# Remainders of at most 64 rows, row indices first, and a tail of nested steps in a kernel for attention and two expert layers

## The chip, the cores and the metric

One core of a Trainium2 chip. The metric is the device time of one execution in microseconds (us); the median of three runs of the kernel before is 681.71 us (680.21 to 682.52).

## The reference

Three layers follow one another. An attention over 2 x 8 heads, 768 positions and 64 features lets a query see the keys of its own hash bucket alone. A feed-forward layer of 1536 tokens (512 to 2048 to 512) has a rational function between its products. The last layer sends each token to the one expert of eight whose logit is highest:

```python
e_idx = np.argmax(logits, axis=1)
for e in range(E):
    mask = e_idx == e
    h = np.maximum(x[mask] @ w1[e], 0.0)
    ye = h @ w2[e]
    out[mask] = gate_w[mask, None] * eom[mask, e, None] * ye
```

w1 is 512 x 1024 and w2 1024 x 512 for each expert. How many tokens an expert gets is known only on the chip.

## The kernel before, in words

Every fp32 operand is split into two fp16 parts, so that one product of the reference is three on TensorE. The operations of attention, the feed-forward layer and the first expert block are recorded in a graph, each with its engine and cost; a planner on the host (order) goes through them in simulated time and emits, per engine, the ready operation with the lowest rank in the table PLACES. What stands behind it, `tail()`, is written out by hand and follows the graph on every engine's queue.

**Routing.** The tokens of an expert are cut into pairs (256 rows, two blocks or subs of 128) and at most one rest. VectorE counts (slots, cum at L872 to L878), makes the matrices SO and SR (L886, L887), and TensorE turns them into row numbers with inv() (L937, L943). idg (L938) is the list for the gathers, idx (L939) that for the scatters, cs_ (L945) the scales. Between these lie the operations that find the expert of each pair and rest (es, L947 to L963; regs is what SyncE loads) and the flags (flf, flc, fli, L964 to L970), two bits for each pair and rest: not empty, and for a rest a second half block of 64 rows, for a pair a new expert.

**Movement.** gather (L984, GpSimd, software queue) fetches rows of x2d into a buffer XG, and a transposing DMA on SyncE (turn, L987) puts it into XGT. Buffers 0 and 1 serve even steps, 2 and 3 odd steps, 4 and 5 the rests. load_chunk (L794, SyncE) brings one of eight chunks (512 KB) of an expert's weights into the staging buffer st; a register from regs picks the expert, and a condition leaves out the load where a pair keeps its expert or a slot is empty. ScalarE and VectorE convert st to the fp16 parts WH (L1002) and WL (L1005), one set for the pairs and one for the rests. Results go out with an indirect scatter on GpSimd (L1042 for a pair's sub, L1117 for a rest); each waits until the one before it has landed.

**The steps.** Pair 0 is in the graph. tail() begins with the rest-0 gather, its eight weight loads and its transpose, then loads fli into registers on every engine. Step k (1 to 9) treats pair k and rest k-1:

```python
gather(k + 1, 0), gather(k + 1, 1); gather_rest(k)
whole(k)          # from k = 3 inside If(pair_over(k, 0)), with an Else
renew(k + 1, 0, 4); load_rest(k, 0, 4)
for sub in range(2): scale_out(k, sub), scatter(k, sub)
If(rest_over(r, 0)): rest(r, 0); If(rest_over(r, 1)): rest(r, 1)
renew(k + 1, 4, 8); load_rest(k, 4, 8)
```

whole(k) converts half of the rest's weights, runs the first products of both subs together with 256 columns (up_pair, 96 matmuls, L1077; relus at L1082 and L1083), issues turns(k) for the next step, converts the other half and runs the second products (mm2s, 48 matmuls of 512 columns, L1034). rest(r, hh) has 96 first products of 64 columns (L1094) and 24 second ones (L1107), then ScalarE and VectorE (L1115, L1116) make its output. Steps above 4 are nested in If(steps > k). renew converts the pair's weights where the expert changes. In this execution five pairs (steps 1 to 5) ran behind pair 0, and rests 0 to 3 in steps 1 to 4, each with its first half block alone.

Of the kernel before, what the change touches and what calls it, by code (L numbers as in the profile page):

```python
# [21 lines left out]
NB, NR = 10, 8  # L22
# [34 lines left out]
    "uiuougusv7u@u@vDuSucu&u<u]u_v5v9vJueu>u|v%v;v#v/v}w4w8xPxrxNxfx%x%x%tjtpr#r(r;r?r{s2s4s8sEsAsMsSsYsis!s.t7tJtPtXr^s0s6sCsUsIscsOsysss+s]t1t9tLtTt=u~vBvNq]r3r9rJrhrXrrrxr%rzr*r=r[r}"  # L57
    "smsuvTvZvfwKs&s<s|t3tBtFtHtNtZtRtltxt(t;t{u8wSwgwowqw!w.xVx1y2y8tftvt#t}uGuUukuwu)uyv3vFvRvbvlvtv-w2wEwat*uYumuuu+u:vXvjvvvhv(w0wAwQwewmwww$w<w]uEu$u.vHvVvPv*vpv[v?w6wIwcwuw*w:w~x3"
    "xBxFvnvrvzv=wGwOwywYw@w+x5xHxRxbxlxuxzx#x*x/x?x^y0yCyKyOyQySyWycygymyYyuy+y:yeyky|zfzlz?yqyyy$y$y.y_y_y_ywy!y)y>y<y~zFzFzFzFz7zDzNzTzZznzxzp!4z[!8!C!Gy@y@z3zBzLzRzbzXzjz-z-z-z-zVzV"
    "z#z#z#z#z#z#z%z;wCw&wUx9v1v^wivdwsw_uqwWx7vLwkxhwMxJx-v{w>x=u!w|xXvxxDxxxLxTxZxdxnx(xpxvx;x[x}y4x{y6yAyUyiysy&y]z9zJyEyGyIyMyayoxjz5zHzPzdz*zhztz(z/z^z{z}!0!6!Az=!Ezr!2"  # L60
# [257 lines left out]
def kernel_body(ctx, tc, qt_, kt_, v, proj, wio, ab, wg, w1, w2, cst, out):  # L318
# [398 lines left out]
    def switch():  # L717
# [24 lines left out]
        flf, flc, fli = tp(p2, "flf", [1, 2, NIT]), tp(p2, "flc", [1, 3]), tp(p2, "fli", [1, 3], I32)  # L742
        nc.gpsimd.memset(flf[:, 1, 2 * NR:], 0.0)
# [4 lines left out]
        P["pw"] = pw = tp(p2, "pw", [128, NB - 1])  # L748
        for j in range(NB - 1):
            nc.gpsimd.memset(pw[:, j:j + 1], 4.0**j)  # L750
# [8 lines left out]
        P["csh"], P["idh"] = tp(p2, "csh", [64, 1]), tp(p2, "idh", [64, 1], I32)  # L759
# [64 lines left out]
    def early():  # L824
# [27 lines left out]
        dv(lambda: V.tensor_scalar(out=P["padm"], in0=P["oh8"], scalar1=-1.0, scalar2=128.0, op0=ALU.add, op1=ALU.mult), ["oh8"], ["padm"], 0.08, RT1)  # L852
# [111 lines left out]
    dv(lambda: V.tensor_tensor(out=P["flf"][:, 0, 0:NB - 1], in0=P["es"][:, 2, 1:NB], in1=P["pw"][o1], op=ALU.mult), ["es2b"], ["flf0"])  # L964
    dv(lambda: V.tensor_tensor(out=P["flf"][:, 0, NB - 1:], in0=P["es"][:, 3, 1:NB], in1=P["pw"][o1], op=ALU.mult), ["es3"], ["flf1"])
    for i, p in ((0, 0), (1, 64)):
        dv(lambda i=i, p=p: V.scalar_tensor_tensor(out=P["flf"][:, 1, NR * i:NR * i + NR], in0=PV2[p:p + 1, 2 * NB:NSLOT], scalar=0.0, in1=P["pw"][p:p + 1, 0:NR], op0=ALU.is_lt, op1=ALU.mult), [kPV2], [("flf2", i)])
# [299 lines left out]
```

## Time and profile before

| | |
|---|---|
| median of three runs | 681.71 us (680.21 to 682.52) |
| the profiled execution | 680.25 us |
| its span | 678.5 us |
| mean granted TensorE clock | 0.976 |
| busy: TensorE, VectorE, ScalarE, GpSimd | 583.8, 555.8, 437.8, 272.3 us |

The span runs from the first to the last instruction of the profiled execution. Times in the rows further down are us from its start. PE is TensorE's matmuls, PEld its weight loads, DVE is VectorE, ACT ScalarE, POOL GpSimd, and SPq the DMA queue of SyncE. A granted clock of 1.00 is the higher of TensorE's two levels and 0.50 the lower. The bracket behind a row gives how long the engine had been idle, and what ended it; "issue" is a wait for nothing that the profile shows. Pair 0 ends at about 512, step 1 begins at 522.22, and steps 2 to 5 at 551.56, 580.99, 615.98 and 647.08.

### The profile page before, as it was taken

The page shows a single profiled execution, that of the slowest core. Times are in us where ns is not written, and L with a number is a line of the kernel's source. Part 1 is how long each engine was busy: PE and PEld are TensorE (multiplying, and loading weights), DVE is VectorE, ACT ScalarE, POOL GpSimd, SP SyncE. Part 2 cuts the span into 40 slices and gives each one's busy share as a digit, 9 for nine tenths or more (in the row PEclk, how much of TensorE's full clock was granted, in tenths as well). Part 3 has the DMA queues.
Part 4 walks back from the last instruction along what each step waited for, and adds up shares of the span by engine and source line. Part 5 has one row for each costly group of instructions (what it writes and reads, how often), then busy time and mean ns, then how long its engine had stood idle before and what let it go on. Part 6 is the DMA issues. An engine that isn't in the chain of part 4 may idle for free. (4 is left out here: it accounts for less than half of the span.)

```text
span 678.5 us, 18427 instructions
## 1 busy us (share of the span) xinstructions
PE 583.8 (86%) x7147; PEld 422.2 (62%) x7147; DVE 555.8 (82%) x1185; ACT 437.8 (65%) x644; POOL 272.3 (40%) x218
## 2 busy tenths in 40 slices
PE   0129997999999999999999999999993989797993
PEld 0016775776777776767676777777562666565561
DVE  6999999899999999988999999989962644466452
ACT  4417769797888887978958877765611544365451
POOL 1000215576656737664547554721204031313131
PEclk9999998999999999999999999999997999897998
DMA  7877899799699999998969795745517875997551
GB/s 253 246 227 234 219 228 204 144 157 185 124 161 188 189 207 185 172 157 139 165 134 163 117 172 98 127 79 206 138 48 214 235 266 159 317 296 252 108 102 39
DMA packets 224154, 119.71 MB, mean 176 GB/s; under 512 B 201647, under 2 KB 206639, under 8 KB 224048
## 3 DMA queue, kind: packets, MB, share of 16 engines
q1 hardware_dynamic: 221296, 109.92, 74.4%
q0 software_dynamic: 2752, 8.39, 3.9%
q8 instruction: 64, 1.05, 0.7%
q14 instruction: 42, 0.34, 0.2%
HBM read 82.10 MB, written 6.82 MB: 131 GB/s over the span
## 5 line engine op out<-in xcount | busy, mean ns | idle before, releaser
L313 POOL TENSOR_TENSOR phl<-p,phl 128x768 f16<-128x768 f32 x80 | 136.6, 1714 | 88.7 <-ACT phl L312 49.8
L634 PE MATMUL bank<-XT,WH 128*128 128x128 f16 x1440 | 131.3, 220 | 2.1 <-DVE tmp L655 1.6
L634 PEld LDWEIGHTS <-WH 128*128 128x128 f16 x1536 | 121.1, 98 | 15.5 <-issue 3.2
L634 PE MATMUL bank<-XT,WL 128*128 128x128 f16 x720 | 126.4, 220 | 0.1
L576 ACT ACTIVATE p<-scb,sm 128x768 f32<-128x768 f32 x96 | 93.0, 986 | 21.9 <-DVE sm L570 13.6
L660 PE MATMUL bank<-WH,G 128*128 128x512 f16 x352 | 104.8, 379 | 0.0
L568 DVE TENSOR_REDUCE sm<-scb 128x1 f32<-128x768 f32 x96 | 90.3, 951 | 8.4 <-PE scb L562 6.7
L660 PEld LDWEIGHTS <-G 128*128 128x128 f16 x576 | 52.2, 98 | 51.1 <-POOL G L313 1.4
L1005 DVE SCALAR_TENSOR_TENSOR WL<-st,WH 128x1024 f16<-128x1024 f32 x56 | 65.7, 1230 | 19.3 <-ACT WH L1002 19.3
L1077 PE MATMUL scb<-XGT,WH 128*128 128x256 f16 x320 | 58.6, 290 | 21.6 <-issue 13.6
L634 PEld LDWEIGHTS <-WL 128*128 128x128 f16 x768 | 75.6, 98 | 0.2 <-DVE WL L443 0.2
L313 POOL TENSOR_TENSOR G<-tmp,G 128x512 f16<-128x512 f32 x39 | 47.0, 1206 | 60.7 <-ACT G L312 58.2
L660 PE MATMUL bank<-WL,G 128*128 128x512 f16 x176 | 66.7, 379 | 0.0
L1002 ACT ACTIVATE WH<-st 128x1024 f16<-128x1024 f32 x56 | 54.9, 1046 | 17.1 <-DMA st<-in_w 13.9
L312 ACT ACTIVATE phl<-p 128x768 f16<-128x768 f32 x72 | 60.1, 840 | 7.3 <-DMA pT<-phl 6.4
L1042 POOL DMA_INDIRECT out<-OS,idx x12 | 14.0, 1167 | 114.7 <-ACT OS L1038 96.2
L585 PE MATMUL bank<-VH,pT 128*128 128x65 f16 x528 | 55.3, 195 | 4.3 <-DMA pT<-phl 2.3
L1034 PE MATMUL bank<-WH,HT 128*128 128x512 f16 x192 | 57.3, 379 | 0.6 <-DVE HT L1027 0.6
L585 PEld LDWEIGHTS <-pT 128*128 128x128 f16 x528 | 49.2, 97 | 9.9 <-DMA pT<-phl 6.0
L586 PE MATMUL bank<-VL,pT 128*128 128x64 f16 x528 | 55.3, 192 | 0.0
L587 PE MATMUL bank<-VH,pT 128*128 128x65 f16 x528 | 55.2, 193 | 0.0
L586 PEld LDWEIGHTS <-pT 128*128 128x128 f16 x528 | 48.9, 99 | 4.5 <-issue 0.7
(284 smaller groups left out, 1425.9 us busy)
## 6 DMA issues: line engine op xcount, KB each, us to landing
st<-in_w SPq DMA_DIRECT2D x96, 512.0 KB
tmp<-in_wio SPq DMA_DIRECT2D x32, 512.0 KB
qraw<-in_qt_ SPq DMA_DIRECT2D x12, 256.0 KB
x2d<-X SPq DMA_DIRECT2D x12, 256.0 KB
kraw<-in_kt_ SPq DMA_DIRECT2D x5, 384.0 KB
vr<-in_v SPq DMA_DIRECT2D x5, 384.0 KB
AQ<-BQ SPq DMA_DIRECT2D x24, 64.0 KB
pT<-phl SPq DMA_TRANSPOSE x88
```

The costliest lines, as they stand in the source:

```text
L312: g.op("ACT", c_act(n, 1), lambda: nc.scalar.activation(out=hi, in_=src, func=AF.Copy), r=rd, w=kh, prio=prio, tag=tags[0], alt=[("DVE", c ...
L313: f = lambda e: lambda: e.tensor_tensor(out=lo, in0=src, in1=hi, op=ALU.subtract)
L568: g.op("DVE", 0.865, lambda: nc.vector.tensor_reduce(out=s[:, 0:1], in_=sc, axis=AX.XY, op=ALU.max), r=kb, w=[("mx", ks)], prio=prio, tag= ...
L576: g.op("ACT", 0.975 if ac else 0.885, lambda: nc.scalar.activation(out=pf.rearrange("p (c n) -> p c n", c=2), in_=sc, func=AF.Exp, bias=s[ ...
L585: nc.tensor.matmul(o, lhsT=pt[:, k], rhs=VH[p][:, hh, k], start=(k == 0), stop=False)
L586: nc.tensor.matmul(o[:, 0:D], lhsT=pt[:, k], rhs=VL[p][:, hh, k], start=False, stop=False)
L587: nc.tensor.matmul(o, lhsT=pt[:, 6 + k], rhs=VH[p][:, hh, k], start=False, stop=(k == 5))
L634: nc.tensor.matmul(hp[:, j * 128:j * 128 + 128], lhsT=w_[:, f, d * 128:d * 128 + 128], rhs=xt[:, hl * 4 + d], start=(k == 0), stop=(k == 11))
L660: nc.tensor.matmul(bank_f32(abank), lhsT=G_[:, gl, c0:c0 + 128], rhs=w_[:, f, 512:1024], start=(f == 0 and k == 0), stop=(f == FT - 1 and ...
L1005: nc.vector.scalar_tensor_tensor(out=P["W"][p][1][c], in0=P["st"][c], scalar=512.0, in1=P["W"][p][0][c], op0=ALU.mult, op1=ALU.subtract)
L1034: nc.tensor.matmul(bank_f32(6 + sub), lhsT=P["HT"][sub][:, hl, f], rhs=w_[4 + f // 2][:, c0:c0 + 512], start=(f == 0 and n == 0), stop=(f ...
L1077: nc.tensor.matmul(scb[half][:, f // 2, (f % 2) * 256:(f % 2) * 256 + 256].rearrange("p (s r) -> p s r", s=2), lhsT=w_[2 * half + f // 2][ ...
```

## The change

A rest holds at most 64 rows (padm 64 for 128), so rest() has one half block and no inner If; a larger remainder becomes a pair. The flags become four numbers: a mask of pairs with a new expert, the number of rests, of pairs, and of steps; they no longer depend on PV2, and are loaded within the graph (a TensorE operation for the planner, emitted on all engines). The table PLACES ranks the chain to idg and idx, and the first gather of step 1, ahead of expert and flag operations, and sub 0 of step 1 ahead of sub 1 in gather and transpose. Gather buffers XG are 0 and 1 for pair 0, and 2 and 3 for all later pairs (XGT keeps its alternation). Step 1 issues gather(2) first, then gather and transpose of rest 0, then its weight loads. whole(1) runs its first products block by block as pair 0 does, with 128 columns (4 x 48 matmuls), all relus ahead of the conversions of rest 0, and the transposes behind; mm2s goes sub by sub in every step. Steps 3 and 4 have no If around whole(k). Both scatters of step k and its load_rest(k, 4, 8) move to the start of the branch of step k + 1; where no step follows, the scatters stand in that If's Else. NB goes from 10 to 12 and NR from 8 to 7.

```diff
...
-NB, NR = 10, 8
+NB, NR = 12, 7
...

...
-        flf, flc, fli = tp(p2, "flf", [1, 2, NIT]), tp(p2, "flc", [1, 3]), tp(p2, "fli", [1, 3], I32)
-        nc.gpsimd.memset(flf[:, 1, 2 * NR:], 0.0)
+        flf, flc, fli = tp(p2, "flf", [1, NB - 1]), tp(p2, "flc", [1, 4]), tp(p2, "fli", [1, 4], I32)
...
-        P["pw"] = pw = tp(p2, "pw", [128, NB - 1])
+        P["pw"] = pw = tp(p2, "pw", [1, NB - 1])
...
-            nc.gpsimd.memset(pw[:, j:j + 1], 4.0**j)
+            nc.gpsimd.memset(pw[:, j:j + 1], 2.0**j)
...

...
-        dv(lambda: V.tensor_scalar(out=P["padm"], in0=P["oh8"], scalar1=-1.0, scalar2=128.0, op0=ALU.add, op1=ALU.mult), ["oh8"], ["padm"], 0.08, RT1)
+        dv(lambda: V.tensor_scalar(out=P["padm"], in0=P["oh8"], scalar1=-1.0, scalar2=64.0, op0=ALU.add, op1=ALU.mult), ["oh8"], ["padm"], 0.08, RT1)
...

...
-    dv(lambda: V.tensor_tensor(out=P["flf"][:, 0, 0:NB - 1], in0=P["es"][:, 2, 1:NB], in1=P["pw"][o1], op=ALU.mult), ["es2b"], ["flf0"])
-    dv(lambda: V.tensor_tensor(out=P["flf"][:, 0, NB - 1:], in0=P["es"][:, 3, 1:NB], in1=P["pw"][o1], op=ALU.mult), ["es3"], ["flf1"])
-    for i, p in ((0, 0), (1, 64)):
-        dv(lambda i=i, p=p: V.scalar_tensor_tensor(out=P["flf"][:, 1, NR * i:NR * i + NR], in0=PV2[p:p + 1, 2 * NB:NSLOT], scalar=0.0, in1=P["pw"][p:p + 1, 0:NR], op0=ALU.is_lt, op1=ALU.mult), [kPV2], [("flf2", i)])
-    dv(lambda: V.scalar_tensor_tensor(out=P["flc"][:, 2:3], in0=P["tot"][:, 0:1], scalar=1.0, in1=P["tot"][:, 1:2], op0=ALU.add, op1=ALU.max), ["tot"], ["flc2"])
-    dv(lambda: V.tensor_reduce(out=P["flc"][:, 0:2], in_=P["flf"], axis=AX.X, op=ALU.add), ["flf0", "flf1", ("flf2", 0), ("flf2", 1)], ["flc"])
-    dv(lambda: V.tensor_copy(P["fli"], P["flc"]), ["flc", "flc2"], ["fli"])
+    dv(lambda: V.tensor_tensor(out=P["flf"], in0=P["es"][:, 3, 1:NB], in1=P["pw"], op=ALU.mult), ["es3"], ["flf"])
+    dv(lambda: V.tensor_copy(P["flc"][:, 1:3], P["tot"]), ["tot"], ["flc1"])
+    dv(lambda: V.scalar_tensor_tensor(out=P["flc"][:, 3:4], in0=P["tot"][:, 0:1], scalar=1.0, in1=P["tot"][:, 1:2], op0=ALU.add, op1=ALU.max), ["tot"], ["flc2"])
+    dv(lambda: V.tensor_reduce(out=P["flc"][:, 0:1], in_=P["flf"], axis=AX.X, op=ALU.add), ["flf"], ["flc"])
+    dv(lambda: V.tensor_copy(P["fli"], P["flc"]), ["flc", "flc1", "flc2"], ["fli"])
+    flags = []
+
+    def ldflags():
+        flags.extend(nc.values_load_multi_w_load_instructions(P["fli"][0:1, 0:4], min_val=0, max_val=2 ** NB - 1)[1])
+    g.op("PE", 1.0, ldflags, r=["fli"], w=["flags"], prio=RT)
...

...
-    def turn_in(i):
-        nc.sync.dma_start_transpose(out=P["XGT"][i], in_=P["XG"][i].rearrange("p a b -> p (a b)"))
+    def turn_in(o, i):
+        nc.sync.dma_start_transpose(out=P["XGT"][o], in_=P["XG"][i].rearrange("p a b -> p (a b)"))
     def gather(k, sub):
-        gather_to(2 * (k % 2) + sub, 2 * k + sub)
+        gather_to(2 * min(k, 1) + sub, 2 * k + sub)
     def turn(k, sub):
-        turn_in(2 * (k % 2) + sub)
+        turn_in(2 * (k % 2) + sub, 2 * min(k, 1) + sub)
     def gather_rest(r):
...
     def turn_rest(r):
-        turn_in(4 + r % 2)
+        turn_in(4 + r % 2, 4 + r % 2)
     def conv_hi(p, c):
...

...
-                    nc.tensor.matmul(b_[:, f], lhsT=w_[2 * half + f // 2][:, c0:c0 + 128], rhs=x_[:, hl * 4 + d, 64 * hh:64 * hh + 64], start=(n == 0), stop=(n == 11))
+                    nc.tensor.matmul(b_[:, f], lhsT=w_[2 * half + f // 2][:, c0:c0 + 128], rhs=x_[:, hl * 4 + d, 0:64], start=(n == 0), stop=(n == 11))
...
-    def rest(r, hh):
+    def rest(r):
...
-        up_rest(r, hh, 0), up_rest(r, hh, 1)
+        up_rest(r, 0), up_rest(r, 1)
...
-        lo, hi = slice(0, 64), slice(64, 128)
-        sc, at_ = P["cs_"][lo, s:s + 1], P["idx"][lo, s:s + 1]
-        if hh:
-            nc.vector.tensor_copy(P["csh"], P["cs_"][hi, s:s + 1])
-            nc.vector.tensor_copy(P["idh"], P["idx"][hi, s:s + 1])
-            sc, at_ = P["csh"], P["idh"]
-        hb, os = P["HB"], P["OS"][2][lo]
-        nc.scalar.activation(out=hb, in_=bank_f32(5)[hi, :], func=AF.Copy, scale=sc)
-        nc.vector.scalar_tensor_tensor(out=os, in0=bank_f32(5)[lo, :], scalar=sc, in1=hb, op0=ALU.mult, op1=ALU.add)
-        nc.gpsimd.indirect_dma_start(out=out[:, :], out_offset=bass.IndirectOffsetOnAxis(ap=at_, axis=0), in_=os, in_offset=None, bounds_check=NT - 1, oob_is_err=False)
+        sc = P["cs_"][0:64, s:s + 1]
+        hb, os = P["HB"], P["OS"][2][0:64]
+        nc.scalar.activation(out=hb, in_=bank_f32(5)[64:128, :], func=AF.Copy, scale=sc)
+        nc.vector.scalar_tensor_tensor(out=os, in0=bank_f32(5)[0:64, :], scalar=sc, in1=hb, op0=ALU.mult, op1=ALU.add)
+        nc.gpsimd.indirect_dma_start(out=out[:, :], out_offset=bass.IndirectOffsetOnAxis(ap=P["idx"][0:64, s:s + 1], axis=0), in_=os, in_offset=None, bounds_check=NT - 1, oob_is_err=False)
...

...
         def load_rest(r, c0, c1):
-            if r < NR - 1:
+            if r < NR:
...
         def conv(p, c0, c1):

...
         def conv_rest(r, c0, c1):
-            if r < NR - 1:
+            if r < NR:
                 conv(1, c0, c1)
         def turns(k):
...
-            if k < NR - 1:
+            if k < NR:
...
-        gather_rest(0)
-        load_rest(0, 0, 8)
-        turn_rest(0)
-        _, (f_pair, f_rest, steps) = nc.values_load_multi_w_load_instructions(P["fli"][0:1, 0:3], min_val=0, max_val=4 ** (NB - 1) - 1)
-
-        def pair_over(k, n):
-            return (f_pair & (3 << 2 * (k - 1))) > (n << 2 * (k - 1))
-
-        def rest_over(r, n):
-            return (f_rest & (3 << 2 * r)) > (n << 2 * r)
+        f_new, n_rest, n_pair, steps = flags
         def renew(k, c0, c1):
...
-                with tc.If(pair_over(k, 1)):
+                with tc.If((f_new & (1 << (k - 1))) > 0):
                     conv(0, c0, c1)
         def whole(k):
...
-            conv_rest(r, 0, 4)
-            load_pair(k + 1, 0, 4)
-            up_pair(k, 0)
-            turns(k)
-            up_pair(k, 1)
+            if k > 1:
+                conv_rest(r, 0, 4)
+                load_pair(k + 1, 0, 4)
+                up_pair(k, 0)
+                turns(k)
+                up_pair(k, 1)
+            else:
+                for sub in range(2):
+                    for half in range(2):
+                        mm1(k, sub, half), relu_hi(k, sub, half), relu_lo(k, sub, half)
+                conv_rest(r, 0, 4)
+                load_pair(k + 1, 0, 4)
+                turns(k)
             conv_rest(r, 4, 8)
             load_pair(k + 1, 4, 8)
-            for half in range(2):
-                for sub in range(2):
+            for sub in range(2):
+                for half in range(2):
...
         def without(k):
-            r = k - 1
-            conv_rest(r, 0, 8)
+            conv_rest(k - 1, 0, 8)
...
             load_pair(k + 1, 4, 8)
-        with ExitStack() as es_:
-            for k in range(1, NB):
-                r = k - 1
-                if k > 4:
-                    es_.enter_context(tc.If(steps > k))
-                if k + 1 < NB:
-                    gather(k + 1, 0), gather(k + 1, 1)
-                if k < NR - 1:
-                    gather_rest(k)
-                if k < 3:
+        def scatters(k):
+            scatter(k, 0), scatter(k, 1)
+
+        def step(k):
+            r = k - 1
+            if k + 1 < NB:
+                gather(k + 1, 0), gather(k + 1, 1)
+            if k == 1:
+                gather_rest(0), turn_rest(0)
+                load_rest(0, 0, 8)
+            if k < NR:
+                gather_rest(k)
+            if k < 5:
+                whole(k)
+            else:
+                with tc.If(n_pair > k) as full:
...
-                else:
-                    with tc.If(pair_over(k, 0)) as full:
-                        whole(k)
-                    with full.Else():
-                        without(k)
-                renew(k + 1, 0, 4)
-                load_rest(k, 0, 4)
-                for sub in range(2):
-                    scale_out(k, sub), scatter(k, sub)
-                if r < NR - 1:
-                    with tc.If(rest_over(r, 0)):
-                        rest(r, 0)
-                        with tc.If(rest_over(r, 1)):
-                            rest(r, 1)
-                renew(k + 1, 4, 8)
-                load_rest(k, 4, 8)
+                with full.Else():
+                    without(k)
+            renew(k + 1, 0, 4)
+            load_rest(k, 0, 4)
+            scale_out(k, 0), scale_out(k, 1)
+            if r < NR:
+                with tc.If(n_rest > r):
+                    rest(r)
+            renew(k + 1, 4, 8)
+
+        def steps_from(k):
+            step(k)
+            if k + 1 == NB:
+                scatters(k)
+            elif k < 4:
+                load_rest(k, 4, 8), scatters(k), steps_from(k + 1)
+            else:
+                with tc.If(steps > k + 1) as more:
+                    load_rest(k, 4, 8), scatters(k), steps_from(k + 1)
+                with more.Else():
+                    scatters(k)
+
+        steps_from(1)
...
```

## Rows read from the trace of the kernel before

**Rows 1.** First products: stretch, us, PE busy (count), PEld busy, PEclk, DMA share, GB/s.
```profile
522.22:534.54 12.32, 12.32 (x96) 10.14 (x95) 0.85 1.06 347
647.08:657.55 10.47, 10.47 (x96) 9.29 (x96) 1.00 0.46 108
```

**Rows 2.** TensorE in order of time: start, us, line, op [idle before <- releaser].
```profile
522.22 0.58 PE L1077 MATMUL scb<-XGT,WH 128*128 128x256 f16 x2 [9.64 <-issue]
...
551.56 0.38 PE L1077 MATMUL scb<-XGT,WH 128*128 128x256 f16 x2 [0.98 <-DMA st<-in_w]
...
554.60 0.38 PE L1077 MATMUL scb<-XGT,WH 128*128 128x256 f16 x2 [1.25 <-issue]
...
580.99 0.38 PE L1077 MATMUL scb<-XGT,WH 128*128 128x256 f16 x2 [1.14 <-DMA st<-in_w]
...
584.53 0.58 PE L1077 MATMUL scb<-XGT,WH 128*128 128x256 f16 x2 [2.72 <-issue]
...
615.98 0.58 PE L1077 MATMUL scb<-XGT,WH 128*128 128x256 f16 x2 [4.17 <-DMA st<-in_w]
...
647.08 0.38 PE L1077 MATMUL scb<-XGT,WH 128*128 128x256 f16 x2 [1.68 <-DVEq L1207]
```

**Rows 3.** Half clock: us, busy PE, PEld, DVE, ACT, POOL, PEclk, DMA, GB/s.
```profile
584.05:587.47 3.42, 2.94 (x15) 2.02 (x14) 3.07 (x3) 1.25 (x2) 2.88 (x2) 0.50 0.89 277
614.77:621.60 6.83, 5.62 (x27) 3.94 (x28) 6.83 (x7) 5.96 (x7) 1.00 (x1) 0.50 0.78 253
```

**Rows 4.** VectorE in order of time, the row indices.
```profile
505.06 0.28 DVE L950 TENSOR_REDUCE es<-es 1x18 f32<-1x144 f32 x1
...
508.70 0.68 DVE L1027 SCALAR_TENSOR_TENSOR HT<-scb,HT 128x512 f16<-128x512 f32 x1
...
509.30 0.18 DVE L938 TENSOR_SCALAR idg<-bank 128x28 int32<-128x28 f32 x1
```

**Rows 5.** GpSimd's gathers (L984) and scatters in order of time.
```profile
509.75 1.04 POOL L984 DMA_INDIRECT XG<-x2d,idg  x1 [3.13 <-DVE regs L957]
...
517.13 0.99 POOL L984 DMA_INDIRECT XG<-x2d,idg  x1 [1.77 <-issue]
...
555.30 0.91 POOL L1117 DMA_INDIRECT out<-OS,idx  x1 [6.44 <-issue]
...
585.98 2.06 POOL L984 DMA_INDIRECT XG<-x2d,idg  x1 [0.34 <-issue]
...
666.55 1.03 POOL L1042 DMA_INDIRECT out<-OS,idx  x1 [12.40 <-ACT OS L1038]
...
670.11 1.00 POOL L1042 DMA_INDIRECT out<-OS,idx  x1 [2.54 <-DMA out<-OS,idx]
```

**Rows 6.** SyncE's queue in order of time: transposes and weight loads.
```profile
513.14 3.28 SPq L987 DMA_TRANSPOSE XGT<-XG  x2
...
518.54 4.90 SPq L794 DMA_DIRECT2D st<-in_w  x8
...
594.38 4.64 SPq L987 DMA_TRANSPOSE XGT<-XG  x2
```

**Rows 7.** TensorE's weight loads in order of time, ahead of step 1.
```profile
520.61 0.11 PEld L1077 LDWEIGHTS <-WH 128*128 128x128 f16 x1 [8.13 <-DMA XGT<-XG]
...
522.25 0.10 PEld L1077 LDWEIGHTS <-WH 128*128 128x128 f16 x1 [1.54 <-issue]
```

**Rows 8.** TensorE in order of time, 24 products of pair 0, the first and the next.
```profile
504.21 0.28 PE L1019 MATMUL scb<-XGT,WH 128*128 128x128 f16 x2
...
505.55 0.59 PE L1034 MATMUL bank<-WH,HT 128*128 128x512 f16 x2
```

**Rows 9.** Stretches: step 3 and the end.
```profile
581.00:616.00 35.00, 28.10 (x265) 18.91 (x266) 20.44 (x22) 19.52 (x25) 8.09 (x5) 0.93 0.98 308
668.20:678.50 10.30, 0.00 (x0) 0.00 (x0) 0.00 (x0) 0.66 (x1) 1.00 (x1) 0.72 0.17 57
```

**Rows 10.** VectorE in order of time, conversions of step 4.
```profile
614.13 9.17 DVE L1005 SCALAR_TENSOR_TENSOR WL<-st,WH 128x1024 f16<-128x1024 f32 x8 [0.78 <-ACT WH L1002]
```

More of the change, by code (lines that the diff above doesn't have):

```diff
@@ L56 @@
     "rNrfsqquq+r5rDrHrmrvr/sws)s:s>s_t0t5tdp5pJpNpZprpxp#p=p{p/q8qGqQqYqxq!rjrprtsGp?qEqKqaqsqiq>q)q~r1rBrLrVrbrnr.sKsQsWsasgsos$s@tDtVtbthtntrtzt-t?t[u0u4ttt^u2u6t%t/uCuKuOuWuAuIuMuQua"
[L57 to L60, printed above, removed]
+    "uiuougusv9u@u]vFuSucu&u<u_u|v7vBvLueu>u~v(v=v%v;w0w6wAxRxtxPxhx(x*x-tjtpr#r(r;r?r{s2s4s8sEsAsMsSsYsis!s.t7tJtPtXr^s0s6sCsUsIscsOsysss+s]t1t9tLtTt=v1vDvPq]r3r9rJrhrXrrrxr%rzr*r=r[r}"
+    "smsuvVvbvhwMs&s<s|t3tBtFtHtNtZtRtltxt(t;t{u8wUwiwqwsw$w:xXx3y8yEtftvt#t}uGuUukuwu)uyv5vHvTvdvnvvv/w4wGwct*uYumuuu+u:vZvlvxvjv*w2wCwSwgwowyw&w>w_uEu$u.vJvXvRv-vrv^v[w8wKwewww-w<x1x5"
+    "xDxHvpvtv#v?wIwQw!waw]w.x7xJxTxdxnxwx#x%x;x?x{y0y6yIyQyUyWyYycyiymysyey!y>y]ykyqz7zfzj!Mywy&y+y.y@z1z3z5y$y)y<y|y_z9zJzLzNzPzDzHzVzZzbzlzr!A!Y!C!c!g!kztzvzxzzz#z%z(z*z-z/z;z=z?z[z^"
+    "z{z}!0!2!4!6!8wEw)wWxBv3v{wkvfwuw|uqwYx9vNwmxjwOxLx=v}w@x^u!w~xZvzxFxzxNxVxbxfxpx/xrxxx[x}y4yAy2yCyGyayoyyy:y~zFzTyKyMyOySygyuxlzBzRzXzd!Gzhzp!E!I!O!Q!S!U!a!ezn!W!K!i"
 )
@@ L758, in switch @@
         P["HTR"], P["HB"] = tp(p2, "HTR", [128, 2, 8, 64], F16), tp(p2, "HB", [64, DM])
-        P["csh"], P["idh"] = tp(p2, "csh", [64, 1]), tp(p2, "idh", [64, 1], I32)
         P["OS"] = [tp(p2, f"OS{i}", [128, DM]) for i in range(3)]
@@ L1083, in up_pair, with up_rest @@
             nc.vector.scalar_tensor_tensor(out=h_[1], in0=b_, scalar=0.0, in1=h_[0], op0=ALU.max, op1=ALU.subtract)
-    def up_rest(r, hh, half):
+    def up_rest(r, half):
         Wh, Wl = P["W"][1]
```

## The prediction

> **What bounds it now.** The change touches only the routing and the expert tail, from about 502 us to the end. I went through the views in this order: the list of TensorE's instructions in time, for where its idle stretches lie; the table of stretches, for the clock and the DMA load in them; then the lists of GpSimd, SyncE and VectorE, for what each idle stretch waits on.
>
> In the tail TensorE's own work sets the time. One step without a pause is 96 first products (10.47 us at full clock [rows 1]), the second products and the rest. What is not work stands in seven idle stretches [rows 2]: 9.64 us ahead of step 1, then 0.98 and 1.25 around the start of step 2, 1.14 and 2.72 around that of step 3, 4.17 ahead of step 4 and 1.68 ahead of step 5. The last six sum to 11.94 us. They all lie between a rest and the next first products, or just inside these. No other place in the pair and rest stages shows one, and the releasers named (a weight load whose chunks these products don't read, issue, a queue) are no tile of theirs. What stands in that place in the program is the inner If on a second half block: not taken in any of the four rests, it skips 120 matmuls and their 120 weight loads. So I read these six as the cost of that skip: the end of the stage is drained, and the code behind it has to come in. Two are followed by half clock, 584.05 to 587.47 and 614.77 to 621.60, with 2.94 and 5.62 us of busy TensorE in them [rows 3].
>
> The 9.64 us ahead of step 1 are a chain. The row indices idg come at 509.30 behind a relu of 0.68 us [rows 4], the gathers for step 1 at 509.75 and later [rows 5], their two transposes at 513.14 and after [rows 6], and the weight load that needs the second of them waits 8.13 us, until 520.61 [rows 7]. Behind it 1.54 us more go to the flags, which every engine loads there [rows 7]; GpSimd shows the same pause as 1.77 us ahead of 517.13 [rows 5].
>
> **Part by part.** The slots, pairs and rests keep their number on this input: the rests hold few rows, since no rest entered its second half. So the work on TensorE is the same but for the form in step 1.
>
> *Step 1 starts earlier.* Ten small VectorE operations for experts and flags leave the stretch ahead of idg, and the relu goes behind it: 0.6 us for the relu, and 0 to 1.8 us for operations of at most 0.28 us like the one at 505.06 [rows 4], of which part filled pauses. I take 1.2 in all, so the first gather at 508.5. Its transpose follows after 3.4 us as now (509.75 to 513.14) and SyncE's flags are loaded by then; landing takes 4.5 to 6 (the second, behind the first on SyncE at some 514.5, stands at 520.6), and I take 4.5 for one with nothing beside it: 516.4. With blocks of one half (sub 0 first) TensorE no longer needs the second transpose to begin, and the flags lie ahead of this point. I take 516.8 against 522.22: -5.4 us, with bounds -7 and -3. The flags now hold up the end of pair 0, some 2 us on TensorE, which has 9.64 us of cover here; without it they would cost these 2.
>
> *Blocks for up_pair.* 192 products of 128 columns stand for 96 of 256. 24 of them take 504.21 to 505.55, or 0.056 each [rows 8]: 10.7 us, against 12.32 now at clock 0.85, and 10.47 at full clock [rows 1]. The pause ahead of them shrinks to some 1 or 2 us, so I take full clock: -1.6, bounds 0 and -1.6.
>
> *Weights of rest 0 come later.* Eight loads go out from 518.54 for 4.90 us [rows 6]. They now stand on SyncE behind the transpose of rest 0, that one behind its gather, and that one on GpSimd behind both gathers of step 2, which wait for both transposes of step 1, as they write the buffers these read. The second lands near 520.5; gather, landing, transpose issue and the two register loads make 527.5 of it, 9 us later than now. 4.2 MB at the 308 GB/s of 581 to 616 [rows 9] take 13.6: last landing near 543 with a latency of 2, converted near 545.3, rest 0 ends near 546.7. Without this wait it would end at 543.5 (550.58 - 7.0). So +3.2, bounds 0 and +6. The three parts make -3.8 at the end of rest 0.
>
> *The inner If goes.* -11.94 us of idle, less what the remaining branches cost. No row shows a bare branch; the smallest of the stretches, 0.98, is a ceiling, 0 the floor. I take 0.3 at each of four step ends: -10.7. The half clock goes with the pauses: half of 2.94 + 5.62 us: -4.3. Bounds together -16.2 and 0.
>
> *Given back in steps 3 and 4.* In step 4 eight conversions of 9.17 us stand on VectorE ahead of its relus, from 614.13, 2.3 us after rest 2's end at 611.8 [rows 10]. They end 11.5 us after it, the first products 10.8: 0.7 us late, and 0.7 more for a relu. Besides, GpSimd now issues a step's two scatters after the rest's scatter and ahead of the next gathers, each waiting for the landing before it. A landing costs 2.54 us when nothing else runs (ahead of 670.11), and up to 6.44 in the loads (ahead of 555.30) [rows 5]. The gathers in step 3 came 6.1 us after the rest's end (579.85 to 585.98); they will come 1.4 + 2 x 2.54 to 2 x 6.44 + 1 = 7.5 to 15.3 after it. SyncE keeps transposes and weight loads in one queue, so the loads of pair 4 and rest 3 slip with them. I take +2.9 for that, +4.3 in all; bounds 0 and +10.
>
> *Nothing for the rest.* Dropped flag operations and the plain compares lie beside TensorE's work. The last two scatters move into an Else behind a far jump; GpSimd is idle 12.40 us ahead of the first of them [rows 5], which covers even a stretch like 4.17. Without that cover it would be +4.2. The last stretch of 10.30 us [rows 9] stays.
>
> The Trainium skill (Runtime: NRT & Kernel Launch, Instruction fetch mechanics) says that fetch runs in sequence and that a taken branch out of the fetched window waits for its code. By that, the six idle stretches go with the skip, as taken here, and the far jump ahead of the last scatters gets one of its own; uncovered, the sum would be 4.2 us higher.
>
> **Sum:** -5.4 - 1.6 + 3.2 - 10.7 - 4.3 + 4.3 = -14.5. The profiled execution took 680.25 us (span 678.5, 1.75 around it), so 665.7 by its own time. It lies 1.46 under the median of 681.71; against the median I forecast **667 us**. All gains whole and nothing given back: 658.5.
>
> **Rivals.** *B, the queue of gathers binds.* For: from a gather at 585.98 to the first transpose at 594.38 went 8.4 us, 4.64 more to issue both [rows 5, 6], and some 3.2 to land (at most 4.2, from 516.4 to 520.6 in step 1): 16.2. With landings of 6.44 the tiles are ready 31.5 us after a rest, against 26.6 of work (615.98 to 647.08 less 1.68 and 2.8 of half clock): 4.9 us of wait at each of three steps, 14.7 instead of the 4.3: 681.7 - 18.8 + 14.7 = 677.6. Against: DMA is less loaded elsewhere, and at 2.54 each there is no wait. Between them, 673 to 678.
>
> By the Trainium skill (DMA: Bandwidth & Descriptors, Anatomy of one DMA — SWDGE path) a transfer costs about 2.0 us and its bytes at 436 GB/s, an estimate of 2.6 for a scatter of 256 KB. The 2.54 agrees, the 6.44 does not; by the page B would not happen.
>
> *C, the idle stretches stay.* If they belong to the outer Ifs, or to code that comes in late in any case, only step 1's gain is left: -3.8, 678. For: 1.25 and 2.72 lie inside the first products, behind the jump. Against: stretches without an inner If show nothing like it.
>
> The Trainium skill (same page on the runtime and section) gives TensorE a store of 2,048 instructions. With a window that large, 240 skipped ones would need no fetch, and C would follow; 4.17 us after one skip speaks against it.
>
> *D, slower.* The place is B's: GpSimd's scatters ahead of the gathers. If a landing takes 7.9 us instead of 6.44, as with both weight sets under way, tiles stand 34.4 us after a rest: 7.8 us at three steps, 23.4, over the 18.8 of gains: 686. It is slower from about 7.2 us a landing. The longest row, 6.44, speaks against it.
>
> **Numbers.** Main case 0.57 (658 to 671), B 0.25, C 0.10, D 0.08. The range 658 to 678 leaves out D and the outer ends of B and C. About 0.3% (2 us) can be told from no change. Faster: the main case, B and half of C, 0.87; same 0.05; slower 0.08.
>
> **What would show it.** TensorE's first product of step 1 near 517 at clock 1.0; a pause of 1 to 4 us ahead of or in rest 0; step starts without stretches over 0.5 us, no half clock from 530 to 660; gathers 11 us after each rest's end; the second products of step 4 some 4 us late. Wrong, if stretches labelled issue remain after the rests (C), or first products wait for the transposed tile in steps 3 to 5 (B, D).

## The result and the profile after

The changed kernel takes 670.38 us (median of four, 669.22 to 672.75), the kernel before 681.07 beside it: a ratio of 0.9845 [0.981, 0.9881], 10.7 us less. The forecast was 667 within 658 to 678. The profiled execution took 669.22 us, span 667.4 (before: 680.25 and 678.5), mean clock 0.985.

The parts ahead of the routing are the same work in both, and vary by some us between executions. So in what follows I also use the time from the routing's first comparison on VectorE (L872 before, L870 after) to the end of the span: 175.9 us before, 166.9 after. 2.1 of the 11.1 us between the two spans lie ahead of that point.

TensorE in order of time (start, us, line, op, idle before and its releaser); these are all its idle stretches over 0.2 us from step 1 on, and the starts of steps 3 and 5 as examples of those that have none:

```profile
514.18 0.27 PE L1020 MATMUL scb<-XGT,WH 128*128 128x128 f16 x2 [2.27 <-DMA XGT<-XG]
...
543.23 1.10 PE L1108 MATMUL scb<-WH,HTR 128*64 128x512 f16 x4 [5.01 <-ACT HTR L1098]
...
574.69 0.39 PE L1078 MATMUL scb<-XGT,WH 128*128 128x256 f16 x2
...
589.13 0.61 PE L1035 MATMUL bank<-WH,HT 128*128 128x512 f16 x1 [3.78 <-ACT HT L1083]
...
590.37 0.61 PE L1035 MATMUL bank<-WH,HT 128*128 128x512 f16 x1 [0.63 <-DVE HT L1084]
...
620.48 0.39 PE L1035 MATMUL bank<-WH,HT 128*128 128x512 f16 x1 [0.85 <-DVE HT L1084]
...
636.24 0.39 PE L1078 MATMUL scb<-XGT,WH 128*128 128x256 f16 x2
```

The seven stretches of [rows 2] have become other ones. Step 1 starts at 514.18 behind 2.27 us instead of 9.64, and none of the step starts has a stretch any more. New are 5.01 us inside rest 0, 3.78 + 0.63 ahead of and among the second products of step 3, and 0.85 in step 4. Behind the two long ones the clock falls, as it did behind the stretches of before [rows 3] (us, then busy PE, PEld, DVE, ACT, POOL, then PEclk, DMA share, GB/s):

```profile
538.20:548.30 10.10, 5.09 (x26) 2.00 (x26) 3.65 (x5) 3.34 (x6) 0.00 (x0) 0.66 0.74 146
588.40:595.20 6.80, 5.44 (x13) 1.91 (x14) 5.16 (x8) 4.64 (x8) 2.96 (x3) 0.53 1.02 412
```

ScalarE and SyncE's queue in order of time show what the two wait for:

```profile
540.40 1.06 ACT L1003 ACTIVATE WH<-st 128x1024 f16<-128x1024 f32 x1 [1.73 <-DMA st<-in_w]
...
541.64 1.26 ACT L1039 ACTIVATE OS<-bank,cs__7394 128x512 f32<-128x512 f32 x2 [0.18 <-ACTq L1148]
...
542.79 0.66 ACT L1098 ACTIVATE HTR<-bank 128x256 f16<-128x256 f32 x2
...
581.33 1.06 ACT L1003 ACTIVATE WH<-st 128x1024 f16<-128x1024 f32 x1 [5.79 <-DMA st<-in_w]
...
588.48 0.60 ACT L1083 ACTIVATE HT<-scb 128x512 f16<-128x512 f32 x1
```

```profile
525.21 5.06 SPq L792 DMA_DIRECT2D st<-in_w  x8
...
536.29 3.73 SPq L988 DMA_TRANSPOSE XGT<-XG  x2
...
566.48 3.86 SPq L988 DMA_TRANSPOSE XGT<-XG  x2
...
573.16 1.23 SPq L988 DMA_TRANSPOSE XRT<-XG  x1
...
577.95 2.83 SPq L792 DMA_DIRECT2D st<-in_w  x4
...
650.86 3.75 SPq L988 DMA_TRANSPOSE XGT<-XG  x2
```

The loads of rest 0 go out at 525.21; before, they went at 518.54 [rows 6]. The last chunk is converted at 540.40, 2.8 us after the seventh where those before it came some 1.3 us apart; transposes for step 2, which start at 536.29, stand beside it. Then come two scale_outs (1.26 us), and only then the relu that TensorE waits for since 538.22. In step 3 the conversion of rest 2's first chunk starts at 581.33 after 5.79 us of wait for its load, and four of them stand ahead of the relus of the pair (588.48). That load went out at 577.95. Ahead of it on SyncE stand the transposes of step 2, the last of which waited until 573.16 for its gather, and four loads of pair 3 that the condition leaves out (0.07 to 0.08 us each from 574.74 on; 5 GB/s are moved from 576.30 to 577.90). On GpSimd, in order of time:

```profile
561.24 0.99 POOL L1043 DMA_INDIRECT out<-OS,idx  x1 [3.27 <-ACT HT L1083]
...
562.54 1.47 POOL L985 DMA_INDIRECT XG<-x2d,idg  x1 [0.30 <-issue]
...
587.84 1.51 POOL L985 DMA_INDIRECT XG<-x2d,idg  x1 [0.31 <-issue]
...
653.88 1.57 POOL L1043 DMA_INDIRECT out<-OS,idx  x1 [3.40 <-ACT OS L1039]
...
661.72 1.00 POOL L1043 DMA_INDIRECT out<-OS,idx  x1 [6.27 <-DMA out<-OS,idx]
```

The gathers come at 562.54 and 587.84, 14.2 and 13.1 us after the rests' ends (548.30, 574.76); before it was 6.1 in step 3 [rows 5]. Each stands behind two scatters that wait for the landings ahead of them.

### The profile page after: what moved, and what is told of

The parts are those of the page before. It is cut to its first block, busy times and chain, and to the rows that moved or that the text cites. A ratio compares the mean times of both kernels' runs of the same rounds, so it can differ in the third digit from the quotient of the medians.

```text
span 667.4 us, 18493 instructions
## 1 busy us (share of the span) xinstructions
PE 580.8 (87%) x7243; PEld 419.3 (63%) x7243; DVE 557.8 (84%) x1183; ACT 438.8 (66%) x644; POOL 273.2 (41%) x219
## 4 chain that ended last, share of the span: by engine, by line
DVE 37%; DMA 20%; issue 16%; ACT 12%; PE 11%; POOL 3%; POOLq 0%; SPq 0%; DVEq 0%; ACTq 0%
DMA out<-OS,idx 10%; DVE sm L568 7%; DMA pT<-phl 5%; ACT p L576 3%; DVE tmp L648 3%; ACT phl L312 3%; DVE tmp L440 2%; PE bank L660 2%; DVE tmp L649 2%; DVE WL L443 2%; DVE tmp L441 2%; DVE tmp L650 2%; DVE tmp L653 2%; DVE tmp L655 2%; DVE bank L654 2%
## 5 line engine op out<-in xcount | busy, mean ns | idle before, releaser
L634 PE MATMUL bank<-XT,WH 128*128 128x128 f16 x1440 | 129.6, 219 | 2.1 <-DVE tmp L655 1.5
L634 PE MATMUL bank<-XT,WL 128*128 128x128 f16 x720 | 124.9, 219 | 0.2 <-DVE sm L569 0.2
L576 ACT ACTIVATE p<-scb,sm 128x768 f32<-128x768 f32 x96 | 93.0, 986 | 21.3 <-DVE sm L570 13.6
L1003 ACT ACTIVATE WH<-st 128x1024 f16<-128x1024 f32 x56 | 56.5, 1049 | 21.6 <-DMA st<-in_w 21.3
L1035 PE MATMUL bank<-WH,HT 128*128 128x512 f16 x192 | 59.8, 392 | 5.8 <-ACT HT L1083 3.8
L1035 PEld LDWEIGHTS <-HT 128*128 128x128 f16 x288 | 28.2, 100 | 40.6 <-issue 4.3
L562 PE MATMUL scb<-AK,AQ 128*128 128x384 f16 x192 | 46.8, 326 | 5.8 <-ACT p L576 5.2
```

The lines of the kernel that those rows point to most:

```text
L576: g.op("ACT", 0.975 if ac else 0.885, lambda: nc.scalar.activation(out=pf.rearrange("p (c n) -> p c n", c=2), in_=sc, func=AF.Exp, bias=s[ ...
L634: nc.tensor.matmul(hp[:, j * 128:j * 128 + 128], lhsT=w_[:, f, d * 128:d * 128 + 128], rhs=xt[:, hl * 4 + d], start=(k == 0), stop=(k == 11))
L1003: nc.scalar.activation(out=P["W"][p][0][c], in_=P["st"][c], func=AF.Copy, scale=512.0)
L1035: nc.tensor.matmul(bank_f32(6 + sub), lhsT=P["HT"][sub][:, hl, f], rhs=w_[4 + f // 2][:, c0:c0 + 512], start=(f == 0 and n == 0), stop=(f ...
```

## The experiments

Every ratio is to the kernel before measured beside it, with its 95% interval. The last two columns are of the one profiled execution, whose time can lie some us off the median.

| kernel | median, us | ratio | profiled, us | routing to end, us |
|---|---|---|---|---|
| before | 681.1 | 1 | 680.25 | 175.9 |
| changed | 670.4 | 0.9845 [0.981, 0.9881] | 669.22 | 166.9 |
| before, no inner If | 663.7 | 0.9736 [0.9675, 0.9796] | 662.25 | 161.0 |
| before, code moved by 128 instructions | 674.4 | 0.9896 [0.9863, 0.9929] | 677.44 | 174.7 |
| changed, inner If back | 671.6 | 0.9866 [0.9818, 0.9914] | 672.22 | 168.8 |
| changed, small inner If | 672.0 | 0.9883 [0.9812, 0.9954] | 673.31 | 173.7 |
| changed, up_pair in step 1 | 669.0 | 0.9787 [0.9734, 0.9839] | 672.31 | 168.2 |
| changed, flags late | 670.9 | 0.9877 [0.9836, 0.9919] | 670.08 | 167.3 |
| changed, rest 0 first | 666.3 | 0.974 [0.9691, 0.979] | 671.74 | 163.8 |
| changed, scatters in the old place | 664.4 | 0.9751 [0.9702, 0.9799] | 667.27 | 163.8 |
| changed, gathers first | 660.6 | 0.9655 [0.9598, 0.9712] | 661.11 | 157.0 |
| rest 0 and gathers first | 656.8 | 0.9665 [0.9633, 0.9698] | 652.86 | 151.1 |
| the same with the inner If | see below | 0.9696 [0.9649, 0.9743] | 666.34 | 159.8 |

The theory: the skip of the inner If made the stretches at the step starts, and the moved scatters and the late loads of rest 0 gave part of it back. The rivals: the stretches come from elsewhere; the waits come from shorter steps or from DMA bandwidth and not from the order.

### The inner If alone

```diff
-                        with tc.If(rest_over(r, 1)):
-                            rest(r, 1)
```

> The kernel before with nothing changed but the inner If on a second half block, which is gone. If the skip of its 240 instructions makes the idle stretches at the step starts, the six stretches (11.94 us) and the half clock behind two of them (4.3) go, step 1 still starts near 522, and the time is 665 to 668. If the stretches belong to the outer Ifs or to code that comes late in any case, they stay, and the time is 680 to 682.

Measured: 663.69 us, 0.9736 [0.9675, 0.9796]. All idle stretches of TensorE over 0.2 us from step 1 on, in order of time:

```profile
519.02 0.59 PE L1077 MATMUL scb<-XGT,WH 128*128 128x256 f16 x2 [9.58 <-issue]
...
612.19 0.39 PE L1034 MATMUL bank<-WH,HT 128*128 128x512 f16 x1 [0.57 <-ACT HT L1082]
...
613.43 0.39 PE L1034 MATMUL bank<-WH,HT 128*128 128x512 f16 x1 [0.85 <-DVE HT L1083]
```

The six stretches are gone, the 9.6 us ahead of step 1 stay. From routing to end it is 14.9 us less than before; the prediction's two terms had made it 15.0. And this one edit is worth more than the whole change: the rest of the change costs some 6 us (161.0 to 166.9). (The edit leaves out the second half block of a rest, which this input never has.)

### The inner If put back, whole and small

```diff
                 with tc.If(n_rest > r):
                     rest(r)
+                    with tc.If(n_rest > r + 16):
+                        rest(r)
```

The small one has `up_rest(r, 0)` as its body. Neither body runs.

> The changed kernel with an inner If, never taken, of a whole further rest behind each rest. If the skip makes the idle stretches, they come back at the starts of steps 2 to 5, 10 to 12 us in all, with half clock behind one or two; part of that is covered where step 3 waits for weights anyway: 678 to 685. If not, 669 to 672.

> As with the inner If put back, but with the first half of a rest's first products (48 matmuls and their weight loads, 96 instructions) as its body. If what costs is to bring in the code behind a long skip, the stretches are under half of those with the whole body: 671 to 675. If it is the branch and the drained engines, they are the same: 678 to 685.

Measured: 671.58 (0.9866 [0.9818, 0.9914]) and 671.97 us (0.9883 [0.9812, 0.9954]); the ratios can't be told from the changed kernel's. Neither time means what its expectation made of it. The first lies in the range for "the skip does not make the stretches", over 6 us under the other one, and yet every one of these step starts has a stretch again, of about 1 us. The second lies in the range for a cost that follows the length, but the stretches are as long as with the whole body. The starts of steps 2 to 5 with the whole body, in order of time:

```profile
550.06 0.38 PE L1078 MATMUL scb<-XGT,WH 128*128 128x256 f16 x2 [1.02 <-ACTq L1203]
...
577.53 0.38 PE L1078 MATMUL scb<-XGT,WH 128*128 128x256 f16 x2 [0.97 <-ACTq L1203]
...
611.45 0.38 PE L1078 MATMUL scb<-XGT,WH 128*128 128x256 f16 x2 [1.00 <-ACTq L1203]
...
639.59 0.38 PE L1078 MATMUL scb<-XGT,WH 128*128 128x256 f16 x2 [1.17 <-ACTq L1203]
```

and step 3's start and the largest stretch of all with the small one:

```profile
573.23 0.38 PE L1078 MATMUL scb<-XGT,WH 128*128 128x256 f16 x2 [0.91 <-ACTq L1203]
...
620.77 0.61 PE L1035 MATMUL bank<-WH,HT 128*128 128x512 f16 x1 [6.44 <-ACT HT L1083]
```

A skip brings 0.9 to 1.3 us at a step start, with 240 instructions or 96 (step 4 with the small body waited 3.05 us, for its transposed tile). The length of the body doesn't set it. The long stretches of 1.25 (in the middle of products), 2.72 and 4.17 us did not come back with the whole body. With the whole body the four stretches sum to 4.2 us, and only 1 to 2 of these appear in the time: the waits in rest 0 and step 3 shrink to 4.14 and 3.51 us. In the execution with the small body the wait for weights fell on step 4 instead (6.44).

### The same code in another place

```diff
+        for _ in range(64):
+            nc.tensor.matmul(bank_f32(5)[:, 0:2], lhsT=P["W"][0][0][0][:, 0:128], rhs=P["W"][0][0][0][:, 0:2], start=True, stop=True)
         gather_rest(0)
```

> The kernel before, inner If and all, with 64 products of 2 columns on TensorE at the head of the tail, in its wait for step 1: they compute nothing that is used and move all code behind them by 128 instructions. If the long stretches (1.25 after 15 products, 2.72 after 6, 4.17 after none) are code that has to come in because the skip lands near or past the end of a piece of code, they go, and only the 0.9 to 1.3 us of the skip itself stay at each of four step starts: 668 to 672. If the skip costs by its length or by the drained engines alone, nothing moves: 679 to 682.

Measured: 674.44 us, 0.9896 [0.9863, 0.9929], from ten runs between 667.7 and 680.3. The starts of steps 2 to 5, in order of time:

```profile
554.40 0.59 PE L1077 MATMUL scb<-XGT,WH 128*128 128x256 f16 x2 [3.91 <-PEq L1209]
...
584.08 0.38 PE L1077 MATMUL scb<-XGT,WH 128*128 128x256 f16 x2 [1.65 <-DMA st<-in_w]
...
614.27 0.38 PE L1077 MATMUL scb<-XGT,WH 128*128 128x256 f16 x2 [3.68 <-DMA st<-in_w]
...
643.77 0.38 PE L1077 MATMUL scb<-XGT,WH 128*128 128x256 f16 x2 [1.32 <-ACTq L1209]
```

Neither expectation held whole. The stretches inside the products (1.25 after 15 of them, 2.72 after 6 [rows 2]) are gone, as the first one said, but step 2 now has 3.91 us and step 4 still 3.68; the sum is 10.6 for 11.9. So in one profiled execution of each the same skip over the same body costs between 1 and 4 us, and the places that cost more moved with the code. The time is less clear: by its ratio this kernel is 7.1 us faster than the kernel before, its ten runs spread over 12.6 us, and the profiled one, the third longest, is only 1.2 us shorter from the routing to the end. Where the others gain the rest is not shown.

The If's own branches on TensorE's queue show part of the wait. Here they take 4.60, 2.01, 3.98 and 0.33 us behind rests 0 to 3, in the order of the four stretches; with the whole body in the changed kernel none takes over 0.42. The two views, here and there (count, then the shortest, median and longest in ns):

```profile
L1209 PEldq COMPARE_BRANCH  x8: 176/262/4602, 548.9 to 642.6; - x8
...
L1203 PEldq COMPARE_BRANCH  x8: 179/262/416, 544.6 to 638.6; - x8
```

In the kernel before, none takes over 1.51 us, so there the 4.17 lie behind the branch and not in it. That these stretches are code being fetched behind a taken branch is the reading that fits the 15, 6 and no products of before, with the steps nearly equal in length, and the shift; it is not shown. The DMA views list an instruction transfer on queue q8 in the windows of the 2.72, 3.68, 3.91 and 4.17 us, but one also beside the 1.32 and the 1.68.

### Step 1 and rest 0

```diff
-                for sub in range(2):
-                    for half in range(2):
-                        mm1(k, sub, half), relu_hi(k, sub, half), relu_lo(k, sub, half)
+                up_pair(k, 0), up_pair(k, 1)
```

> The changed kernel with up_pair (256 columns, both transposes needed) for the first products of step 1 in place of the four blocks. Step 1 starts some 2 us later, near 516. If the weights of rest 0 bind there, rest 0 ends where it did and the time is 669.5 to 671.5; if TensorE's own start binds, 672 to 673.

Measured: 669.04 us, 0.9787 [0.9734, 0.9839]. Step 1 starts 15.1 us after the routing's first comparison, for 13.8 in the changed kernel and 19.7 before. The blocks bring 1.4 of the 5.9 us, and the time doesn't get worse without them: rest 0's weights bind, and the wait in it shrinks to 2.07 us.

For the flags, `ldflags()` was taken out of the graph and called at the head of `tail()`:

```diff
+        ldflags()
         f_new, n_rest, n_pair, steps = flags
```

> The changed kernel with the flags loaded at the head of the tail again, in place of within the graph. If the flags' load on TensorE waits for the transposes issued ahead of it, as the order of before suggests, step 1 starts 1.5 to 3.5 us later, and rest 0's weights, which bind there, take that up: 669 to 672. If the flags cost nothing in either place, step 1 starts 13.7 to 13.9 us after the first comparison of the routing, as in the changed kernel.

Measured: 670.88 us, 0.9877 [0.9836, 0.9919]; step 1 starts 13.6 us after the first comparison. The second expectation holds: it is the same in either place. But the edit doesn't bring back the order of before. There TensorE loaded the flags at 521.2, between the tile (520.61 [rows 7]) and the first product (522.22), 1.6 us in all; here it has loaded them by 511.2, and in the changed kernel by 509.5, ahead of the wait for the tile in both.

So of the 5.9 us of earlier start 1.6 are the flags that are there sooner, 1.4 the blocks, and 2.9 the second tile: its transpose goes out 12.0 us after the first comparison both before and with up_pair in step 1, and the tile is there 6.1 us later before, 3.1 with up_pair. Why it lands sooner was not taken apart. idg comes 0.7 us earlier (6.76 to 6.10 after the first comparison), of which nothing is left at that transpose.

```diff
             if k == 1:
                 gather_rest(0), turn_rest(0)
                 load_rest(0, 0, 8)
+            if k + 1 < NB:
+                gather(k + 1, 0), gather(k + 1, 1)
             if k < NR:
                 gather_rest(k)
```

(the two gathers stood ahead of `if k == 1`)

> The changed kernel with gather, transpose and weight loads of rest 0 issued ahead of the gathers of step 2. If late loads make the 5.0 us wait inside rest 0 and the half clock behind it, both go and the time is 663 to 665, with step 1 still starting near 514. If the wait comes from elsewhere (the order on ScalarE, or the last chunk held up by the transposes of step 2), 669 to 671.

Measured: 666.33 us, 0.974 [0.9691, 0.979]. The wait in rest 0 is gone, the one in step 3 is not; the first stretches behind step 1's start, in order of time:

```profile
559.86 0.39 PE L1035 MATMUL bank<-WH,HT 128*128 128x512 f16 x1 [0.72 <-DVE HT L1084]
...
590.65 0.61 PE L1035 MATMUL bank<-WH,HT 128*128 128x512 f16 x1 [4.37 <-ACT HT L1083]
...
591.89 0.61 PE L1035 MATMUL bank<-WH,HT 128*128 128x512 f16 x1 [0.63 <-DVE HT L1084]
```

Step 2 starts 42.1 us after the first comparison for 47.8. The median is 1 to 3 us more than expected. In the profiled execution, itself 5.4 us over the median, the first products of step 1 ran at half clock for a while (12.5 us for 10.9), and the end took 1 us longer.

### The scatters

```diff
             if k < NR:
                 gather_rest(k)
+            if k > 1:
+                scatters(k - 1)
...
-                load_rest(k, 4, 8), scatters(k), steps_from(k + 1)
+                load_rest(k, 4, 8), steps_from(k + 1)
```

> The changed kernel with the scatters of step k-1 issued behind the gathers of step k on GpSimd. If the scatters' landings hold up gathers, transposes and with them the weight loads of rest 2, the wait of 4.4 us in step 3 and the half clock behind it (3.2) go: 662 to 665. If the loads wait for staging buffers or for DMA bandwidth, 669 to 671.

Measured: 660.61 us, 0.9655 [0.9598, 0.9712], 1.9% under the changed kernel by the ratios, more than expected. TensorE's stretches over 0.3 us behind step 1's start, in order of time:

```profile
544.44 0.86 PE L1108 MATMUL scb<-WH,HTR 128*64 128x512 f16 x4 [3.52 <-ACT HTR L1098]
...
600.82 0.86 PE L1108 MATMUL scb<-WH,HTR 128*64 128x512 f16 x4 [1.51 <-ACT HTR L1098]
...
615.43 0.39 PE L1035 MATMUL bank<-WH,HT 128*128 128x512 f16 x1 [0.79 <-DVE HT L1084]
```

The wait ahead of step 3's second products is gone. SyncE's queue shows why: the first load of rest 2's weights goes out at 570.09, 5.4 us before step 3 starts (575.49); in the changed kernel it went at 577.95, 3.3 us after that start (574.69). In both it stands behind the transposes of step 2 and the four loads left out:

```profile
564.99 1.25 SPq L988 DMA_TRANSPOSE XRT<-XG  x1
...
570.09 3.71 SPq L792 DMA_DIRECT2D st<-in_w  x4
```

Besides, the end got shorter: 7.1 us from the last second products to the end of the span, for 10.1.

> The changed kernel with both scatters of a step back behind its scale_outs, as before the change. If the move of the scatters is what makes the loads of rest 2 late, the wait of 4.4 us in step 3 and the half clock behind it go: 662 to 665. If the loads are late because the steps are shorter, they stay: 669 to 671.

The edit puts `scatter(k, 0)` and `scatter(k, 1)` behind their scale_outs and takes them out of the branches. Measured: 664.35 us, 0.9751 [0.9702, 0.9799]. Step 3 has no wait; rest 0 keeps one of 2.64 us, step 2 has 0.79, and 2.11 and 0.85 us stand in step 4:

```profile
614.70 0.39 PE L1035 MATMUL bank<-WH,HT 128*128 128x512 f16 x1 [2.11 <-ACT HT L1083]
...
615.93 0.61 PE L1035 MATMUL bank<-WH,HT 128*128 128x512 f16 x1 [0.85 <-DVE HT L1084]
```

These two edits undo the wait of step 3 in two ways, with steps as short as in the changed kernel. So it was the order on GpSimd, and neither the shorter steps nor the bandwidth.

### Both orders, and the inner If in them

> Gathers ahead of the scatters and rest 0 ahead of the gathers of step 2, both in one. If the wait in rest 0 and the wait in step 3 are two waits with two causes, their gains add up: 4 to 5 us under the kernel with gathers first alone (660.6), 654.5 to 657.5. If the earlier loads of rest 0 only hold up the transposes of step 2, 659 to 662.

> Rest 0 first and gathers first again, with more rounds, as the fastest version found: 655 to 658, 3.2 to 4 per cent under the kernel before.

Measured: 656.97 us (0.9664 [0.9609, 0.9719]) and in a second set of runs 656.77 (0.9665 [0.9633, 0.9698]), 1.8% under the changed kernel by the ratios. All idle stretches over 0.3 us from step 1 on in the second set's profile, in order of time:

```profile
513.61 0.27 PE L1020 MATMUL scb<-XGT,WH 128*128 128x128 f16 x2 [2.18 <-DMA XGT<-XG]
...
553.13 0.39 PE L1035 MATMUL bank<-WH,HT 128*128 128x512 f16 x1 [0.35 <-DVE HT L1084]
...
607.01 0.39 PE L1035 MATMUL bank<-WH,HT 128*128 128x512 f16 x1 [0.79 <-DVE HT L1084]
```

The two waits had two causes: with both gone, routing to end is 151.1 us, 15.8 less than in the changed kernel. But that profile is of the shortest of its six runs, 3.9 us under their median, and the ratios don't show that the gains add up: against gathers first alone (0.9655) the interval leaves no difference that can be told. The last two scatters of a pair are 4.4 us apart now, where they were 7.8 apart:

```profile
640.57 1.36 POOL L1043 DMA_INDIRECT out<-OS,idx  x1 [3.25 <-ACT OS L1039]
...
644.93 0.98 POOL L1043 DMA_INDIRECT out<-OS,idx  x1 [2.99 <-ACTq L1148]
```

The transposes of a sixth step that never runs stood beside them at 650.86 in the changed kernel; here they are through earlier, at 630.05.

> The fastest version (rest 0 first, gathers first) with the never-taken inner If of a whole rest behind each rest. Put into the changed kernel the same If brought 4.2 us of idle at four step starts and only some 1 us of time. If the waits for weights took the difference, it costs its full 4 to 5 us here, where hardly a wait is left: 660 to 663. If it costs little wherever the code falls well, 657 to 659; if long stretches come back with the code in another place, 665 to 672.

Measured: 666.34, 661.3 and 657.16 us, 0.9696 [0.9649, 0.9743], some 2 us over 0.9665, with intervals that overlap. A fourth execution took 1551.2 us; no row says why, and the ratio leaves it out. In the profiled execution the If brings 0.93, 0.91, 1.00 and 1.17 us at four step starts, two of them here, and a wait of 3.61 us in rest 0 that the version without it had not:

```profile
546.02 1.10 PE L1108 MATMUL scb<-WH,HTR 128*64 128x512 f16 x4 [3.61 <-ACT HTR L1098]
...
579.73 0.38 PE L1078 MATMUL scb<-XGT,WH 128*128 128x256 f16 x2 [0.91 <-DMA st<-in_w]
...
607.25 0.38 PE L1078 MATMUL scb<-XGT,WH 128*128 128x256 f16 x2 [1.00 <-ACTq L1205]
```

That wait isn't the skip's: rest 0's loads went out some 1.2 us later after the first comparison, and the blocks of step 1 ran at full clock (10.88 us, for 12.51 in the version without the If), so that TensorE was at rest 0 earlier. The order alone doesn't always remove it.

So the cost of the skip itself is about 1 us a step when the code falls well. Whether it is worth 2 or 4 us in all is not settled.

## Why the prediction was right, and where it was off

The forecast of 667 lies 3.4 us under the 670.4. By its own steps, in times between the same rows of the two profiled executions:

| step | forecast | measured |
|---|---|---|
| step 1 starts earlier | -5.4 | -8.0, of which 2.1 ahead of the routing |
| blocks for up_pair | -1.6 | -1.6 |
| weights of rest 0 | +3.2 | +7.4 |
| six stretches and their half clock | -15.0 | -17.2 |
| given back in steps 3 and 4 | +4.3 | +8.6 |
| the end | 0 | -0.3 |
| sum | -14.5 | -11.1 |

That the sum came so near is partly luck. The errors of single terms are 8.5 us one way and 5.1 the other, 2.1 of these from the parts ahead of the routing, which the change doesn't touch. Two terms lie outside their own bounds, rest 0 (+6) and the stretches (-16.2).

*Step 1* was right in size (5.9 us by the change), with other parts: I gave 1.2 us to idg, which came 0.7 earlier and left 0.2 at the first transpose and nothing at the second. The flags ahead of the tile (1.6), the tile that lands sooner (3.3 us for the first one, where I took 4.5) and the blocks (1.4) made it up, all three named in the forecast.

*Rest 0* was right in place and mechanism: loads behind the transpose, behind the gathers, behind the transposes of step 1. Its size was the failed term, and not by the landing: counted from the first comparison, the last chunk was converted at 42.3 us (VectorE's half, until 542.72), where the forecast has 42.8. But from there to the end of rest 0 I left 1.4 us, and it took 5.6: the relu stood behind two scale_outs, and behind it came all 24 second products, which the 5.0 us of idle had brought to half clock (5.08 us for 2.78).

*The inner If* was right as a term of this change, and shown by taking it alone out of the kernel before. The reason I gave was too simple. The skip costs about 1 us where it falls well; what made 11.9 of it goes by where the code lies, as the shifted code suggests. That rival C was wrong, the step starts without any stretch show.

*Given back* was right in mechanism (scatters ahead of gathers, SyncE's one queue, loads late), and rival B's place was the right one, though not its wait: no first product waited for its tile. The size was half, and it fell on step 3 and not on step 4: I had looked for the eight conversions of step 4 and not for the four of rest 2 ahead of step 3's relus. Gathers came 10.5 to 16.4 us after the rests' ends, for the 11 forecast. Again the half clock behind the wait (3.2 us) was not in the sum.

*The end* kept its length, but not its work: the first of the last two scatters lands late, beside transposes for a step that never comes. The far jump shows on TensorE, with a branch of 5.35 us behind its last product, where it costs nothing.

Both failed terms have one thing in common: I took the half clock away with every stretch that went, and charged none to the waits that I forecast myself.

## What to carry to other kernels

When an edit sheds waits from a chain, look at what its other parts put into the queues behind it: here a removed branch gave 15 us, and two changes of issue order, each harmless on its own engine, brought waits that cost 16 us between the same rows. Undoing both made the changed kernel 1.8% faster. An indirect scatter that waits for the landing ahead of it does not belong in front of the gathers of the next step, where one more queue (transposes and weight loads) stands behind these. And where a sum forecasts a new wait on TensorE of several us, add what the clock loses behind it.

## What the runs showed of the hardware

A branch over a body that never runs cost TensorE 0.9 to 1.3 us at most step starts, but 1.7, 3.7, 3.9 and 4.2 us at others, with bodies of the same 240 instructions; 1.25 and 2.72 us inside the products of the kernel before come on top. Moving TensorE's code by 128 instructions changed which places these are, in one profiled execution of each. Between 96 and 240 skipped instructions the rows show no difference.

Idle stretches of 5.0 and 3.8 us, inside a rest and ahead of second products, were followed by TensorE's lower level (0.50): the mean granted clock was 0.66 over 10.10 us and 0.53 over 6.80, and the work behind them took 2.3 and 3.2 us longer. Ahead of step 1, 2.2 to 2.4 us of idle did so in some executions (12.5 us for the blocks in the fastest version), while 2.27 us in the changed kernel and 2.89 with the flags late did not (10.9).

The wait of GpSimd for a scatter's landing was 2.5 us with little beside it [rows 5], and 6.1 and 6.3 us beside transposes and weight loads in the changed kernel. The 6.44 of [rows 5] is as long, but that row names no landing.
